# A fused linear-attention and GEGLU block on one core: the first forms of the down projection loaded ahead of two blocks of Wd, the last group's sums in an order of their own, and closings spread with their stores a step later

## The chip, the cores and the metric

The kernel runs on 1 core of a Trainium2 chip. The metric is device time in microseconds (us) of one execution; the times below are the median of 3 runs and their range. The profile is one execution taken by the hardware profiler. Its engines are PE (TensorE matmul; PEld is its weight load), DVE (VectorE), ACT (ScalarE), POOL (GpSimd) and SP (SyncE, which here only issues DMAs).

## The reference

```python
def _A_ref(x, wqkv, wo):            # linear attention, 32 heads of 18
    q, k, v = split_heads(x @ wqkv)
    phi = lambda t: jnp.where(t > 0, t + 1, jnp.exp(t)) + 1e-6
    pq, pk = phi(q), phi(k)
    kv = jnp.einsum("bhsd,bhse->bhde", pk, v)
    z = jnp.einsum("bhsd->bhd", pk)
    num = jnp.einsum("bhqd,bhde->bhqe", pq, kv)
    den = jnp.einsum("bhqd,bhd->bhq", pq, z)[..., None] + 1e-6
    return merge_heads(num / den) @ wo

def _B_ref(x, w_gate, w_up, w_down):
    h = gelu(x @ w_gate) * (x @ w_up)
    return h @ w_down

xn = layernorm(x)                   # x: 2048 x 576, hidden width 4608
return x + _A_ref(xn, ...) * silu(_B_ref(xn, ...))
```

All operands are float32.

## The kernel before

Every float32 product is made of several matmuls on a rounded operand ("hi", written by ACT) and its remainder ("lo", written by DVE as source minus hi).

The program has four stages, one after the other: k and v, then q and the attention output (both up to about 303 us of the profiled execution), then the gate and up matrices, then the down projection. The change lies in the last step of the third stage and in the fourth.

**Gate and up.** A matrix is done in seven block products (`al`, `be`, `ga`, `de`, `al`, `ga`, `de`, line 738), each over two halves of the tokens. Two matrices of two steps each form a *macro group*; there are nine (`NM`), numbered `m` = 0 to 8. A macro group leaves 16 products `h`. They and the sums live in 17 buffers of 128x512, called spots: eight in four `spot_h` tiles, three in `spot_m`, six in `spot_g`. From the products 28 sums are formed on POOL, by the table `ADDS`: an entry `(v, a, b, sign, at)` makes value `v` from `a` and `b`, not before hook `at` of the group. `add_up` (line 827) writes over an operand that nobody needs any more, or takes the spot that came free first. The 26 values named in `FORM` are the *forms*, which are stored to memory (`hs_d`); for the last macro group these stores are issued by POOL itself, right behind the add (`put_out`, line 819), for the others by SP.

**Down projection.** It is done in 26 *passes* (`PROD`). Pass `p` multiplies one form of all nine macro groups (nine steps `kt`) with one combination of blocks of Wd and adds into four PSUM banks: 9 x 4 x 3 = 108 matmuls of 128x288 a pass. The nine steps are cut into five *units* `k` (two steps each, the last one step: macro group 8, which is stored last). Per unit and in this order, `down_all` (line 1135) writes the program: load a third of a Wd block (`load_reg`, passes in `LOADS`), form combinations of Wd blocks on DVE (`change`), split the next pass's weights into hi and lo (`make_words`: ACT, then DVE, tiles `w_head` and `w_end`), split the unit two ahead into hi and lo (`cut`: ACT, then DVE in place on `raw_a`, `raw_b`, `raw_h` or `raw_g`), the matmuls (`down_mm`), then the loads of the same unit for the next pass (`load_unit`, 256 KB each), and in unit 1 the reading of the last pass's banks (`read`). The eight Wd blocks are called by two digits (`"22"`, `"42"`, `"32"`, `"12"`, ...); in the trace a whole one is a `b<-in_wd_dram` load.

**Start of the down projection.** `down_first` (line 1120) lists, for the seven steps of the last up matrix, what is put behind each: four whole blocks of Wd, then the loads of the five units of pass 0, the weights of pass 0 and the first cuts.

**Closings.** Where an output block is complete (`ENDS`: passes 9, 13, 19, 21, 22 twice, 24, 25), `close` does a SiLU on ACT, a multiply and an add on DVE (tile `sx`) and a store to the output, for each of four 128-row parts. From unit 2 of the next pass on, up to three parts are closed a unit. (`run(list, n)` takes the first `n` entries off a list and calls them.)

**Order.** All instructions are kept in the order in which the program writes them on their engine. SP is one queue too: a load whose buffer, source or predecessor isn't ready holds all loads and stores behind it.

Of the kernel before, what the change touches and what calls it, by code (L numbers as in the profile page):

```python
# [49 lines left out]
NM = NG // 2  # L50
# [3 lines left out]
ADDS = (  # L54
# [7 lines left out]
)  # L62

FORM = (33, 18, 11, 19, 31, 27, 29, 15, 30, 25, 6, 43, 40, 42, 35, 17, 4, 26, 39, 24, 41, 22,
# [18 lines left out]
def block_kernel(ctx, tc, x, xe, wq_d, wkv_d, wo, wgu_d, wd_d, out):  # L83
# [12 lines left out]
    def big(i, shape, dt, name):  # L96
        return sb.tile(shape, dt, tag=f"b{i}", bufs=1, name=name)
# [15 lines left out]
    def act(*args, **kw):  # L113
        pin(nc.scalar.activation(*args, **kw))  # L114

    def vec(op, *args, **kw):
        pin(getattr(nc.vector, op)(*args, **kw))  # L117
# [7 lines left out]
    def dma(out, in_, eng=None):  # L125
        tc.keep_in_program_order((eng or nc.sync).dma_start(out=out, in_=in_))
# [277 lines left out]
    def run(todo, n=None):  # L404
        for _ in range(len(todo) if n is None else min(n, len(todo))):
            todo.pop(0)()
# [53 lines left out]
    at = {}  # L460
# [363 lines left out]
    def later(at, f):  # L824
        events.setdefault(at, []).append(f)

    def add_up(m, v, a, b, sign, at):
        into = next((x for x in (a, b) if left[m, x] == 1), None)
        va, vb = value(m, a), value(m, b)
        born(m, v, None if into is None else place_of[m, into])  # L830
        pool("tensor_add" if sign > 0 else "tensor_sub", value(m, v), va, vb)
        for x in (a, b):
            used(m, x, at + 0.5, keep=x == into)
        if v in FORM:
            put_later(m, v, at)
# [7 lines left out]
    def run_events(at):  # L843
        for f in events.pop(at, []):
            f()

    def open_macro(m):
        for v, a, b, sign, at in ADDS:
            at += HOOKS * m
            later(at, lambda a=(m, v, a, b, sign, at): add_up(*a))  # L850

# [50 lines left out]
    def load_reg(at, nm, third=None):  # L902
        if at not in reg:
            b = big(REG[at], [P, REG_W], F32, f"b_{at}")
            reg[at] = b[:, 0 : KT * HALF].rearrange("p (k d) -> p k d", k=KT)
        j, c = int(nm[0]) - 1, int(nm[1]) - 1
        par, f = divmod(KP[j], 2)
        src = wd_d[par::2, :, f, c * HALF : (c + 1) * HALF].rearrange("g p d -> p g d")
        k = slice(0, KT) if third is None else slice(3 * third, 3 * third + 3)
        dma(out=reg[at][:, k], in_=src[:, k])  # L910
# [6 lines left out]
    def raw_place(p, k):  # L917
        if p < 4:
            if k in (0, 1, 4):
                t = ring("a", lambda: big(15, [P, 5, TBN], F32R, "raw_a"))  # L920
            else:
                i = 10 if p == 0 else 6
                t = ring(("b", i), lambda: big(i, [P, 5, TBN], F32R, f"raw_b{i}"))
            return t[:, 4:5] if k == 4 else t[:, 2 * (k % 2) : 2 * (k % 2) + 2]
        if k == 4:
            return ring(("g", p % 2), lambda: gl_tile([P, 1, TBN], f"raw_g{p % 2}", F32R))
        return ring(("h", k), lambda: slot([P, 2, TBN], F32R, f"raw_h{k}"))

    def load_unit(p, k):
        if p >= NP:  # L930
            return
        raw_v[p, k] = v = raw_place(p, k)
        for i in range(*UNITS[k]):
            dma(out=v[:, i - UNITS[k][0]].bitcast(F32), in_=hs_d[i][:, PROD[p][0]])
# [4 lines left out]
    def hi_place(p, k):  # L939
        if k == 4 and p > 2:  # L940
            return ring(("hg", p % 2), lambda: gl_tile([P, 1, TBN], f"hi_g{p % 2}", F32R))
        i = 2 if k == 4 else (4 * p + k) % 3
        if i == 2 and k < 4:
            return beside()[:, 0 : 2 * TBN].rearrange("p (k t) -> p k t", k=2)
        t = ring("hi", lambda: big(0, [P, 5, TBN], F32R, "hi"))
        return t[:, 4:5] if k == 4 else t[:, 2 * i : 2 * i + 2]

    def cut(u):
        p, k = divmod(u, NU)
        if p >= NP:  # L950
            return
        hi, lo = hi_place(p, k), raw_v[p, k]
        hi_v[p, k] = hi
        src = lo.bitcast(F32)
        act(hi, src, AF.Copy)
        vec("tensor_sub", lo, src, hi.bitcast(F32))
# [3 lines left out]
    def word_tiles(p):  # L960
# [34 lines left out]
    }  # L995

    LOADS = {
# [3 lines left out]
    }  # L1001
# [1 line left out]
    def change(p, c):  # L1003
        for nm, a, op, b in CHANGES.get(p, ()):
            r = [reg[x][:, HALVES[c]] for x in (nm, a, b)]
            vec("tensor_add" if op == "+" else "tensor_sub", *r)
# [34 lines left out]
    def acc_of(o):  # L1041
        i, j = ACCS[o]
        if i not in acc_t:
            acc_t[i] = big(i, [P, 2, TT, HALF], F32, f"acc_{i}")
        return acc_t[i][:, j]
# [21 lines left out]
    def places(o):  # L1067
        i, c = divmod(o, 2)
        tb = TP[i]
        cols = slice(c * HALF, (c + 1) * HALF)  # L1070
        rows = lambda j: slice(tb * TBN + j * P, tb * TBN + (j + 1) * P)
        return tb, cols, rows

    def load_sx(o):
# [7 lines left out]
        else:  # L1082
            sxs[o] = [tmp([P, 2, HALF], f"sx_{o}_{j}") for j in range(TT)]
            for j, t in enumerate(sxs[o]):
                dma(out=t[:, 0], in_=s_d[tb][:, j, cols])
                dma(out=t[:, 1], in_=x[rows(j), cols])

    def close(o, j):
        _, cols, rows = places(o)
        y, t = acc_of(o)[:, j], sxs[o][j]  # L1090
        act(y, y, AF.Silu, scale=float(SIGN[o]))
        vec("tensor_mul", t[:, 0], y, t[:, 0])
        vec("tensor_add", t[:, 0], t[:, 0], t[:, 1])
        dma(out=out[rows(j), cols], in_=t[:, 0])

    def close_last(o, j, p, parts):

# [22 lines left out]
    def down_first():  # L1120

        return [
            [lambda: load_reg("22", "22")],
            [lambda: load_reg("42", "42")],
            [lambda: load_reg("32", "32"), lambda: load_reg("12", "12")],
            [lambda: load_unit(0, 0), lambda: load_unit(0, 1), lambda: make_words(0, 0)],
            [
                lambda: load_unit(0, 2), lambda: load_unit(0, 3), lambda: load_unit(0, 4),
                lambda: make_words(0, 1), lambda: cut(0),
            ],  # L1130
            [lambda: cut(1)],
            [],
        ]

    def down_all():
        late = []
        last = NP - 1
        for u in range(NP * NU):
            p, k = divmod(u, NU)
            n = KT * p + 2 * k  # L1140
            for at in sorted(events):
                if at <= H_END + n // 2:
                    run_events(at)
            if p in LOADS and k < 3:
                load_reg(*LOADS[p], k)
            if k == 0:
                for o, e in ENDS.items():
                    if e == p:
                        load_sx(o)
            if k < 2:  # L1150
                change(p + 1, k)
            elif k < 4:
                make_words(p + 1, k - 2)
            cut(u + 2)
            if p == last and k == 2:
                break
            for kt in range(*UNITS[k]):
                down_mm(p, kt, range(TT))
            load_unit(p + 1, k)
            if k == 1 and p:  # L1160
                read(p - 1)
                late += [
                    lambda o=o, j=j: close(o, j) for o, e in ENDS.items() if e == p - 1
                    for j in range(TT)
                ]
            elif k > 1:
                run(late, 3)
        run(late)
        o = next(o for o, e in ENDS.items() if e == last)
        for j in range(TT):  # L1170
            for kt in range(UNITS[2][0], KT):
                down_mm(last, kt, (j,))
            late += close_last(o, j, last, 2 if j == TT - 1 else 1)
            run(late, len(late) - 1)
        run(late)
# [97 lines left out]
    for n in range(3, 2 * TT):  # L1273
# [3 lines left out]
        if n >= TT:  # L1277
            j, c = divmod(n - TT, 2)
# [165 lines left out]
```

## Time and profile before

| | us |
|---|---|
| median of 3 runs | 1499.71 |
| range of the runs | 1496.04 to 1501.43 |
| the profiled execution | 1498.64 |
| its span | 1496.7 |
| PE busy (share of the span) | 1473.3 (98%) |
| DVE busy | 1145.1 (77%) |
| POOL busy | 600.7 (40%) |
| ACT busy | 560.8 (37%) |

A timeline row has the start in us, the duration in us, engine, line, operation, output and inputs, shape and count, and in brackets how long the engine sat idle before it and what ended that. A row of windows has a stretch, its length, the busy time of engines with their instruction counts, the granted PE clock as a share of full speed, the mean busy share of the DMA engines and GB/s.

### The profile page before, as it was taken

What the parts mean: (1) busy time and instruction counts of PE and PEld (TensorE: products, weight loads), DVE (VectorE), ACT (ScalarE), POOL (GpSimd) and SP (SyncE); (2) the same over time, 40 slices, a digit from 0 to 9 for tenths busy, and PEclk for the clock granted to TensorE, in tenths of its full rate; (3) what the DMA queues carried; (4) which work ended last, traced back from release to release, by engine and by line L of the source; (5) the groups of instructions that cost most, each with busy time, mean ns of one, the idle gap of its engine ahead of it and who ended that gap; (6) DMA issues with size and microseconds to landing.
All of it is one profiled execution on the core that took longest, in us unless ns stands there. A gap on an engine that the chain in (4) does not pass through costs nothing.

```text
span 1496.7 us, 21860 instructions
## 1 busy us (share of the span) xinstructions
PE 1473.3 (98%) x8128; PEld 1310.3 (88%) x8128; DVE 1145.1 (77%) x1574; ACT 560.8 (37%) x923; POOL 600.7 (40%) x528
## 2 busy tenths in 40 slices
PE   8999999999999999999999999999999999999997
PEld 7989988988888888888888888888878999999997
DVE  7567466546778788777878878777876978989887
ACT  5434335433223222223233232332234556545553
POOL 4342241125655757655675755667636000000000
PEclk9999999999999999999999999999999999999999
DMA  4425004452242423333152243314297888767875
GB/s 169 181 109 207 6 2 158 150 199 85 92 134 81 145 85 117 123 113 134 50 176 91 92 148 106 119 72 166 81 313 251 279 254 262 240 181 233 291 266 204
DMA packets 115100, 230.62 MB, mean 154 GB/s; under 512 B 10850, under 2 KB 42850, under 8 KB 112946
## 3 DMA queue, kind: packets, MB, share of 16 engines
q1 hardware_dynamic: 112338, 217.17, 42.8%
q0 software_dynamic: 2656, 12.06, 2.1%
q8 instruction: 64, 1.05, 0.3%
q14 instruction: 42, 0.34, 0.1%
HBM read 146.57 MB, written 82.58 MB: 153 GB/s over the span
## 4 chain that ended last, share of the span: by engine, by line
PE 92%; DVE 3%; DMA 2%; POOL 1%; issue 1%; ACT 1%; SPq 0%; DVEq 0%; ACTq 0%; POOLq 0%
PE bd L120 22%; PE ga L738 14%; PE de L738 14%; PE al L738 14%; PE kv L120 8%; PE be L738 7%; PE q L120 4%; PE s L120 4%; DMA raw_a<-hs 1%; PE kv_a L120 1%; PE xt L197 1%; PE d L120 1%; DVE sx L117 1%; DMA hs<-spot_g 0%; DVE acc L117 0%
## 5 line engine op out<-in xcount | busy, mean ns | idle before, releaser
L123 POOL TENSOR_TENSOR sm<-raw 128x384 f32<-128x384 f32 x72 | 76.1, 1057 | 153.5 <-DMA raw<-in_wgu_dram 137.5
L120 PE MATMUL kv<-wkv,xo_B 128*128 128x384 f32 x672 | 126.3, 343 | 1.8 <-POOL wkv L123 0.9
L120 PE MATMUL bd<-w_head,hi 128*128 128x288 f32 x516 | 120.3, 299 | 3.3 <-ACT hi L114 3.3
L117 DVE TENSOR_TENSOR wa<-sm,wa 128x768 fp32r<-128x768 f32 x72 | 93.0, 1292 | 36.1 <-ACT wa L114 35.2
L120 PEld LDWEIGHTS kv<-wkv,xo_B 128*128 128x128 f32 x672 | 117.5, 190 | 3.5 <-POOL wkv L123 1.6
L117 DVE TENSOR_TENSOR wb<-raw,wb 128x256 fp32r<-128x256 f32 (+1 forms) x108 | 106.1, 982 | 7.3 <-ACT wb L114 5.8
L117 DVE TENSOR_TENSOR wa<-raw,wa 128x256 fp32r<-128x256 f32 x72 | 65.0, 903 | 50.7 <-ACT wa L114 47.5
L114 ACT ACTIVATE hi<-raw_h 128x1024 fp32r<-128x1024 f32 x59 | 62.5, 1060 | 97.5 <-PE bd L120 65.5
L120 PEld LDWEIGHTS bd<-w_head,hi 128*128 128x128 f32 x516 | 88.7, 192 | 4.0 <-ACT hi L114 4.0
L120 PE MATMUL bd<-w_end,hi 128*128 128x288 f32 x448 | 89.9, 294 | 0.0
L117 DVE TENSOR_TENSOR raw_h<-raw_h,hi 128x1024 fp32r<-128x1024 f32 x59 | 71.7, 1221 | 22.9 <-ACT hi L114 22.8
L114 ACT ACTIVATE spot_h<-spot_h 128x512 f32<-128x512 f32 x49 | 30.8, 633 | 151.6 <-DVE spot_h L117 151.6
L120 PE MATMUL bd<-w_end,raw_h 128*128 128x288 f32 x264 | 77.9, 295 | 0.0
L114 ACT ACTIVATE u<-al 128x512 f32<-128x512 f32 x72 | 41.0, 592 | 90.1 <-PE al L738 77.6
L114 ACT ACTIVATE wa<-sm 128x1152 fp32r<-128x1152 f32 x36 | 41.8, 1161 | 83.5 <-PE de L738 81.3
L120 PEld LDWEIGHTS bd<-w_end,hi 128*128 128x128 f32 x448 | 71.8, 188 | 0.0
L120 PE MATMUL bd<-beside,raw_h 128*128 128x288 f32 x240 | 70.9, 295 | 0.1
L123 POOL TENSOR_TENSOR spot_h<-spot_h,spot_h 128x512 f32<-128x512 f32 x46 | 63.9, 1395 | 2.9 <-DVE spot_h L117 2.4
L120 PE MATMUL q<-xo_B,wq 128*128 128x512 f32 x240 | 64.1, 395 | 0.0
L738 PE MATMUL ga<-xo_B,wb 128*128 128x512 f32 x252 | 63.2, 390 | 0.5 <-DVE u L117 0.5
L738 PE MATMUL al<-xo_B,wa 128*128 128x512 f32 x252 | 63.0, 389 | 0.0
L738 PE MATMUL ga<-xr_B,wb 128*128 128x512 f32 x252 | 63.0, 389 | 0.0
(247 smaller groups left out, 4097.3 us busy)
## 6 DMA issues: line engine op xcount, KB each, us to landing
raw_h<-hs SPq DMA_DIRECT2D x176, 256.0 KB
raw<-in_wgu_dram SPq DMA_DIRECT2D x36, 768.0 KB
hs<-spot_h SPq DMA_DIRECT2D x90, 256.0 KB
hs<-spot_g SPq DMA_DIRECT2D x80, 256.0 KB
b<-in_wd_dram SPq DMA_DIRECT2D x39, 432.0 KB
hs<-spot_m SPq DMA_DIRECT2D x38, 256.0 KB
raw_g<-hs SPq DMA_DIRECT2D x22, 256.0 KB
b<-in_wd_dram SPq DMA_DIRECT2D x4, 1296.0 KB
```

Source lines behind the costliest of these rows:

```text
L114: pin(nc.scalar.activation(*args, **kw))
L117: pin(getattr(nc.vector, op)(*args, **kw))
L120: pin(nc.tensor.matmul(*args, **kw))
L123: pin(getattr(nc.gpsimd, op)(*args, **kw))
L197: pin(nc.tensor.transpose(xts[n][j][:, k, :], xs[:, j, k * P : (k + 1) * P], ident))
L738: nc.tensor.matmul(o, w[0:rows, wi, :], xop[0:rows, xi, :], start=(start and n == 0), stop=(n == len(PASSES) - 1), skip_group_check=True,)
```

## The change

It has three parts.

1. Two of the four whole Wd blocks leave the head of the SP queue. Block `"32"` (one load) now comes behind the nine loads of pass 0; block `"12"` comes as three thirds in the first three units of pass 1.
2. The last macro group takes its sums from `ADDS_LAST`: the first 14 entries as before, the other 14 in another order and with other hooks.
3. At most two parts are closed a unit, from unit 2 on and also in unit 0 of the following pass; the store of a closed part is put on a list and issued at the end of the next unit, behind that unit's loads.

```diff
+ADDS_LAST = ADDS[:14] + (
+    (28, 14, 22, 1, 27), (25, 11, 20, 1, 29), (35, 7, 25, -1, 29), (21, 14, 15, 1, 30),
...
+)
...
     def open_macro(m):
-        for v, a, b, sign, at in ADDS:
+        for v, a, b, sign, at in ADDS_LAST if m == NM - 1 else ADDS:
...
     LOADS = {
-        2: ("31", "31"), 3: ("41", "41"), 4: ("11", "11"), 5: ("21", "21"),
+        1: ("12", "12"), 2: ("31", "31"), 3: ("41", "41"), 4: ("11", "11"), 5: ("21", "21"),
...
+    stores = []
+
     def close(o, j):
...
-        dma(out=out[rows(j), cols], in_=t[:, 0])
+        stores.append(lambda: dma(out=out[rows(j), cols], in_=t[:, 0]))
...
             [lambda: load_reg("22", "22")],
             [lambda: load_reg("42", "42")],
-            [lambda: load_reg("32", "32"), lambda: load_reg("12", "12")],
+            [],
...
-            [lambda: cut(1)],
+            [lambda: load_reg("32", "32"), lambda: cut(1)],
...
             load_unit(p + 1, k)
+            run(stores)
             if k == 1 and p:
                 read(p - 1)
...
-            elif k > 1:
-                run(late, 3)
+            else:
+                run(late, 2)
         run(late)
+        run(stores)
```

PE executes the same instructions in the same order as before. On SP, at the end of the gate and up stage, the queue before, from the first Wd block to the last load of pass 0 (`hs_79` to `hs_87` are the stored forms of macro groups 0 to 8):

```order
L126 DMA b_8700<-in_wd_dram 128x9x288
L126 DMA b_8720<-in_wd_dram 128x9x288
L126 DMA b_8742<-in_wd_dram 128x9x288
L126 DMA b_8744<-in_wd_dram 128x9x288
L126 DMA raw_a<-hs_79 128x512
L126 DMA raw_a<-hs_80 128x512
L126 DMA raw_a<-hs_81 128x512
L126 DMA raw_a<-hs_82 128x512
L126 DMA raw_b_8792<-hs_83 128x512
```

and of the change:

```order
L134 DMA b_8700<-in_wd_dram 128x9x288
L134 DMA b_8720<-in_wd_dram 128x9x288
L134 DMA raw_a<-hs_79 128x512
L134 DMA raw_a<-hs_80 128x512
L134 DMA raw_a<-hs_81 128x512
L134 DMA raw_a<-hs_82 128x512
L134 DMA raw_b_8788<-hs_83 128x512
L134 DMA raw_b_8788<-hs_84 128x512
L134 DMA raw_b_8788<-hs_85 128x512
L134 DMA raw_b_8788<-hs_86 128x512
L134 DMA raw_a<-hs_87 128x512
L134 DMA b_8820<-in_wd_dram 128x9x288
```

Two whole blocks went from ahead of the first unit to behind the last; one of them (`b_8820`) is seen here, the other follows in thirds.

On POOL, in the last macro group, the sums 23, 40, 25 and 35 with their stores, before (35 is the form that the last unit of pass 2 loads):

```order
L123 TENSOR_TENSOR spot_g_3001<-spot_g_3001,spot_g_2996 128x512
L126 DMA hs_87<-spot_g_3001 128x512
L123 TENSOR_TENSOR spot_g_3001<-spot_m,spot_g_3001 128x512
L126 DMA hs_87<-spot_g_3001 128x512
L123 TENSOR_TENSOR spot_h_2992<-spot_h_2992,spot_g_2999 128x512
L126 DMA hs_87<-spot_h_2992 128x512
L123 TENSOR_TENSOR spot_m<-spot_m,spot_h_2992 128x512
L126 DMA hs_87<-spot_m 128x512
```

and of the change the sums 27, 28 (not stored), 25 and 35:

```order
L131 TENSOR_TENSOR spot_h_2993<-spot_m,spot_h_2993 128x512
L134 DMA hs_87<-spot_h_2993 128x512
L131 TENSOR_TENSOR spot_h_2994<-spot_g_2996,spot_h_2994 128x512
L131 TENSOR_TENSOR spot_g_2997<-spot_h_2992,spot_g_2999 128x512
L134 DMA hs_87<-spot_g_2997 128x512
L131 TENSOR_TENSOR spot_g_2997<-spot_m,spot_g_2997 128x512
L134 DMA hs_87<-spot_g_2997 128x512
```

The store of 35 stood seventh among the stores behind that of 27 and now stands second; 35 is now written into the spot from which 25 has just been stored.

On DVE, in pass 14, around the cut of the first unit of pass 15 (`raw_h` with `hi`), before:

```order
L117 TENSOR_TENSOR sx_1_10746<-sx_1_10746 128x288
L117 TENSOR_TENSOR sx_2_10747<-acc_9218,sx_2_10747 128x288
L117 TENSOR_TENSOR sx_2_10747<-sx_2_10747 128x288
L117 TENSOR_SCALAR w_end_8771<-b_8744,w_end_8771 128x1152
L117 TENSOR_TENSOR raw_h_9328<-raw_h_9328,hi 128x1024
L117 TENSOR_TENSOR sx_3_10748<-acc_9218,sx_3_10748 128x288
```

and of the change:

```order
L125 TENSOR_TENSOR sx_1_10748<-sx_1_10748 128x288
L125 TENSOR_SCALAR w_end_8767<-b_8997,w_end_8767 128x1152
L125 TENSOR_TENSOR raw_h_9330<-raw_h_9330,hi 128x1024
L125 TENSOR_TENSOR sx_2_10749<-acc_9220,sx_2_10749 128x288
L125 TENSOR_TENSOR sx_2_10749<-sx_2_10749 128x288
L125 TENSOR_TENSOR sx_3_10750<-acc_9220,sx_3_10750 128x288
```

The third part's multiply and add went from ahead of that cut to behind it.

3 rows, old and new, of the table ADDS_LAST are left out of this document.

## The prediction, made before the changed kernel was run

> **What bounds the kernel now.** I read the waits of TensorE first, from the last up matrix to the end.
>
> ```profile
> span 1496.7 us, 21860 instructions
> PE bd L120 <- ACT hi L114: 3.3, 2, 2.0
> PE bd L120 <- DVE raw_h L117: 3.3, 3, 2.0
> PE bd L120 <- DVE raw_a L117: 2.4, 4, 0.7
> PE bd L120 <- DVE raw_b L117: 1.0, 1, 1.0
> ```
>
> TensorE is the bound: in the last 404 us it waits only 10.0 us. Nothing ahead of that stretch is edited, so the change can win back these 10.0 us and what hangs on them. The timeline of TensorE says where they lie:
>
> ```profile
> 1101.83 1.75 PE L738 MATMUL de<-xr_T,wb 128*128 128x512 f32 x7
> 1104.93 0.53 PE L120 MATMUL bd<-w_head,hi 128*128 128x288 f32 x2 [1.35 <-ACT hi L114]
> 1106.19 0.40 PE L120 MATMUL bd<-w_head,raw_a 128*128 128x288 f32 x1 [0.73 <-DVE raw_a L117]
> 1109.98 0.40 PE L120 MATMUL bd<-w_head,raw_a 128*128 128x288 f32 x1 [0.34 <-DVE raw_a L117]
> 1114.40 0.40 PE L120 MATMUL bd<-w_head,raw_b 128*128 128x288 f32 x1 [0.97 <-DVE raw_b L117]
> 1150.24 0.40 PE L120 MATMUL bd<-w_end,raw_a 128*128 128x288 f32 x1 [0.59 <-DVE raw_a L117]
> 1153.82 0.85 PE L120 MATMUL bd<-w_head,hi 128*128 128x288 f32 x2 [1.99 <-ACT hi L114]
> 1155.37 0.61 PE L120 MATMUL bd<-w_head,raw_a 128*128 128x288 f32 x1 [0.71 <-DVE raw_a L117]
> 1330.33 0.40 PE L120 MATMUL bd<-w_head,raw_h 128*128 128x288 f32 x1 [0.97 <-DVE raw_h L117]
> 1461.34 0.40 PE L120 MATMUL bd<-w_head,raw_h 128*128 128x288 f32 x1 [2.05 <-DVE raw_h L117]
> 1465.06 0.40 PE L120 MATMUL bd<-w_head,raw_h 128*128 128x288 f32 x1 [0.27 <-DVE raw_h L117]
> ```
>
> There are three places. At the start of the down projection, right behind the last up matrix (which ends at 1103.58), 1.35 + 0.73 + 0.34 + 0.97 = 3.39 us. At the end of pass 2 and start of pass 3, 0.59 + 1.99 + 0.71 = 3.29 us. At passes 15 and 24, 0.97 and 2.05 + 0.27 us. The second place costs more than its waits, as the windows of TensorE show:
>
> ```profile
> 1145.00:1150.00 5.00, 4.65 (x35) 1.00 0.72 238
> 1150.00:1155.00 5.00, 2.44 (x12) 0.82 1.01 359
> 1155.00:1160.00 5.00, 4.63 (x19) 0.50 1.05 405
> 1340.00:1450.00 110.00, 110.00 (x833) 1.00 0.83 268
> ```
>
> Undisturbed, a matmul takes 110/833 = 0.132 us, a pass of 108 of them 14.26 us. In the 15 us from 1145 on, 66 were done, worth 8.7 us; 6.3 us were lost, of which 3.3 us were waits. The other 3.0 us are the clock, which was granted at 0.50 behind the wait.
>
> **Part 1, two blocks of Wd leave the head of the queue.** These rows show why the first unit is late:
>
> ```profile
> b<-in_wd_dram SPq DMA_DIRECT2D x4, 1296.0 KB
> 1084.57 6.75 SPq L126 DMA_DIRECT2D b<-in_wd_dram  x4
> 1084.50:1094.00 9.50, 1.00 0.92 311
> 1094.14 2.09 SPq L126 DMA_DIRECT2D raw_a<-hs  x4
> 1104.00:1106.00 2.00, 1.00 1.05 404
> 1103.82 1.06 ACT L114 ACTIVATE hi<-raw_a 128x1024 fp32r<-128x1024 f32 x1 [10.89 <-DMA raw_a<-hs]
> 1098.20 1.35 DVE L117 TENSOR_TENSOR w_end<-b,w_end 128x1152 fp32r<-128x1152 f32 x1
> ```
>
> Four blocks of 1.33 MB are 5.31 MB; by 1094.0 9.5 us x 311 GB/s = 2.95 MB had moved. So when `raw_a` is issued at 1094.14, 2.36 MB still lie ahead of it, at 404 GB/s 5.8 us; by whole blocks, 2.65 MB are taken away, 6.6 us. The unit landed at 1103.8 and will land at 1097.2 to 1098.0. VectorE is at `w_end` until 1099.55 anyhow and then cuts the unit (the first cut ran from 1104.91, so 1.2 us): ready at 1100.8, 2.8 us ahead of TensorE. The next deadline is the third unit, 4 x 12 matmuls = 6.3 us behind the start: 1109.9. VectorE's order up to it stands in these two rows:
>
> ```profile
> 1108.71 1.22 DVE L117 TENSOR_TENSOR raw_a<-raw_a,hi 128x1024 fp32r<-128x1024 f32 x1
> 1112.50 1.85 DVE L117 TENSOR_TENSOR raw_b<-raw_b,beside 128x1024 fp32r<-128x1024 f32 x1
> ```
>
> Behind the first cut (end 1106.1 before) the second cut began 2.6 us later, and from there to the end of the third cut took 5.6 us. From 1100.8 that makes 1109.0: 0.9 us to spare. So all 3.39 us go; the bounds are 2.5 (this margin is missed by as much) and 3.39. The moved loads cost TensorE nothing: block 32 lies in front of the first unit of pass 1, whose matmuls begin at 1103.58 + 14.26 = 1117.8. All that is queued by then (what is left of the nine loads of pass 0, 2.36 MB in all, and 1.33 MB) takes 3.69/0.404 = 9.1 us from 1094.2, to 1103.4. Block 12 is first needed in pass 3. Uncovered, a block would cost its 3.3 us.
>
> **Part 2, the order of the last sums.** These rows carry the second stall:
>
> ```profile
> SPq L126 <- DMA hs<-spot_m: 9.7, 1, 9.7
> 1145.23 0.32 SPq L126 DMA_DIRECT2D raw_a<-hs  x1
> 1119.19 0.56 POOL L126 DMA_DIRECT2D hs<-spot_h  x1 [0.30 <-POOL spot_h L123]
> 1131.85 0.56 POOL L126 DMA_DIRECT2D hs<-spot_g  x1 [0.57 <-POOL spot_g L123]
> 1136.04 2.06 POOL L123 TENSOR_TENSOR spot_g<-spot_m,spot_g 128x512 f32<-128x512 f32 x1 [3.64 <-DMA hs<-spot_g]
> 1142.83 0.56 POOL L126 DMA_DIRECT2D hs<-spot_m  x1 [0.30 <-POOL spot_m L123]
> 1109.09 0.54 POOL L126 DMA_DIRECT2D hs<-spot_g  x1 [12.92 <-DVE spot_g L117]
> ```
>
> SP reached the last load of pass 2 at 1145.23 - 9.7 = 1135.5 and stood until the store of sum 35, issued at 1142.83, had landed 2.4 us later. Every load of pass 3 was queued behind it. In the new order, behind the store of 27 (1119.19 to 1119.75) come 28 and 25 at 1.4 us, 0.3 us and the store of 25 at 1122.8. Sum 35 is written over 25's spot, so it waits for that store to land: a wait that is new. Row 1136.04 is of this kind, 4.2 us behind its store's issue at 1131.85. So 35 starts at 1127.0, takes 2.1 + 0.3, is issued at 1129.4 and has landed by 1131.8. SP asks for it 3.4 us earlier than before, at 1132.1. Moreover, POOL's first store (1109.09) waited 12.9 us for VectorE, which was held by the first cut; that cut is over some 5.3 us sooner, so 35 lands nearer to 1126.5. The stall of 3.29 us goes, and with it the 3.0 us of low clock. Bounds: the waits 2.7 to 3.29, the clock 0 to 3.0.
>
> By the Trainium skill, page "TensorE: Matmul & The Clock Gate", Part 1, the clock halves after about one idle window of 3.4 us. No single wait here is longer than 1.99 us, so by that rule these waits wouldn't have halved it, and the low stretch could stay; the row has the half clock right behind them, and I go by the row.
>
> What POOL does last moves too, 42 and 29 behind 26 and 30; its wait of 3.64 us on a store (row 1136.04) has a like one at 35, so its end is sooner by the 5.3 us alone. Pass 4's weights and fourth unit wait for the last two stores (a rival below).
>
> **Part 3, the closings.** VectorE is the releaser at passes 15 and 24:
>
> ```profile
> 1325.20 0.45 DVE L117 TENSOR_TENSOR sx<-acc,sx 128x288 f32<-128x288 f32 x1
> 1325.68 0.46 DVE L117 TENSOR_TENSOR sx<-sx 128x288 f32<-128x288 f32 x1
> 1442.87 1.23 DVE L117 TENSOR_TENSOR raw_h<-raw_h,beside 128x1024 fp32r<-128x1024 f32 x1 [2.40 <-ACT beside L114]
> 1460.06 1.22 DVE L117 TENSOR_TENSOR raw_h<-raw_h,hi 128x1024 fp32r<-128x1024 f32 x1
> ```
>
> One closing occupies VectorE 0.86 us (1325.20 to 1326.06). Before pass 15 one less lies ahead of the cut: 0.97 becomes 0.11. Before pass 24 VectorE works without a gap from 1442.87, when it had waited for a load, to the cut at 1460.06. Between them lay 1 + 3 closings, and now 2 + 2: the one saved below is handed in above, and the 2.05 us stay. The cut behind it has two closings ahead instead of three, and the 0.27 us go. Gain 0.86 + 0.27 = 1.1 us, bounds 0 (the closings of unit 0 get in the way of pass 24's later cuts) and 3.3. The stores cost SP the same issues, now behind loads that need not wait for VectorE; the output isn't read again.
>
> **Sum.** 3.39 + 3.29 + 3.0 + 1.1 = 10.8 us. Against the profiled execution, 1498.64, that gives 1487.8. The median shown, 1499.71, is 1.1 us above it, so I forecast 1488.9.
>
> **Rivals.**
> 1. *The clock dip stays or comes elsewhere.* For it: no dip follows the 3.39 us at 1104, so a wait alone doesn't decide it. Against: it begins at the longest wait. The 3.0 us are lost: 1491.9.
> 2. *VectorE becomes the bound in pass 0.* Its margin at the third unit is 0.9 us, and POOL now works in the same microseconds; the same cut took 1.22 and 1.85 us above. If the early start is used up in later waits, 3.39 us are lost, 1492.3.
> 3. *The change doesn't do what it says at sum 35:* SP still stands because of its own new wait, or another late store. Then only 3.39 + 1.1 us come: 1495.2.
> 4. *Slower: pass 4's weights on VectorE.* They are written over the spot of 42, whose store is now the last but one. Even with POOL no earlier than before (its last stores ran to 1155), it is issued by 1153 and lands at 1157; then VectorE needs 1.6 + 0.7 + 1.35 + 1.2 = 4.9 us to the first cut of pass 4, due at 1103.6 + 4 x 14.26 = 1160.6. That is a stall of 1.3 us; POOL 5.3 us earlier, none. It decides only when the store lands over 8 us later still, at 1165: a stall of 9.3 and a low clock of 3.0 exceed the gain. At 1168, 12.3 + 3.0 - 10.8 = 4.5 us slower, 1504.2.
>
> **How the numbers follow.** The forecast 0.60, rival 1 0.15, rival 2 0.13, rival 3 0.07, rival 4 0.05. A measurement of this kernel can tell about 0.3%, 4.5 us, from no change. The forecast and the first two rivals are faster by more; rival 3 lies on the border and is halved: faster 0.91, and with some doubt in my rows 0.89; same 0.06; slower 0.05. The forecast's own range is 1486 to 1491. For 8 in 10, it goes up to 1495.0, which takes in the first two rivals; down to 1485.0, with the 2.05 us gone too and 1.5 us for the spread of the runs shown.
>
> **What would show it.** The first `bd` matmul follows the last `de` without a wait; `hi` of the first unit starts near 1098. The last load of pass 2 isn't held by a store, TensorE has no wait at pass 3, and no window between 1145 and 1165 has a clock of 0.50. The wait at pass 24 is still some 2 us, that of pass 15 about 0.1. Wrong it is if waits of TensorE between 1104 and 1165 still sum to over 2 us, or if the clock falls anywhere else in the down projection.

## The result and the profile after

The changed kernel took 1488.87 us, the median of six runs (1486.08 to 1494.1), against 1500.44 us for the kernel before, six runs beside it (1496.04 to 1501.94): ratio 0.9928, 95% interval 0.9904 to 0.9952. The forecast was 1488.9, the range 1485.0 to 1495.0. The six runs stand in two groups and one outlier: 1486.08, 1486.27, 1486.83; 1490.91, 1491.02; 1494.1. The profiled execution is the one of 1491.02 us, so it shows the changed kernel on one of its worse runs. This is its summary of TensorE's waits in the same stretch as before (us in total, times, longest), and then its timeline:

```profile
span 1489.3 us, 21859 instructions
PE bd L128 <- DVE raw_a L125: 3.3, 2, 2.6
PE bd L128 <- DVE raw_h L125: 2.1, 1, 2.1
```

```profile
1101.87 1.75 PE L746 MATMUL de<-xr_T,wb 128*128 128x512 f32 x7
1103.46 0.42 PE L128 MATMUL bd<-w_head,hi 128*128 128x288 f32 x2
...
1135.09 0.40 PE L128 MATMUL bd<-beside,raw_a 128*128 128x288 f32 x1 [2.61 <-DVE raw_a L125]
1151.90 0.40 PE L128 MATMUL bd<-w_head,raw_a 128*128 128x288 f32 x1 [0.71 <-DVE raw_a L125]
1454.92 0.40 PE L128 MATMUL bd<-w_head,raw_h 128*128 128x288 f32 x1 [2.09 <-DVE raw_h L125]
```

The waits fell from 10.0 us to 5.4. The first one after the last `de` is gone, and so are 0.97 at pass 15 and 0.27 in pass 24. But two stand where the forecast has none: 2.61 us inside pass 2 (which runs from about 1132 to 1151) and 0.71 at the start of pass 3, 3.32 us in all, as much as the 3.29 us that were to vanish there. Behind the first of them the clock falls. These windows show all five engines, in the order PE, PEld, DVE, ACT, POOL, and then the clock, the DMA share and GB/s:

```profile
1130.00:1135.00 5.00, 2.48 (x19) 2.24 (x17) 5.00 (x3) 1.06 (x1) 4.06 (x6) 1.00 0.88 291
1135.00:1140.00 5.00, 4.91 (x25) 4.91 (x26) 4.48 (x3) 0.29 (x1) 4.36 (x5) 0.66 0.80 288
```

A mean of 0.66 over 5 us, between 1.00 and 0.50, is 0.34/0.5 x 5 = 3.4 us at half clock. Before, it was 0.18/0.5 x 5 = 1.8 us in one window and all 5 us of the next, 6.8 us at the second stall. VectorE, the third of these columns, works without a pause from 1130 to 1135 while TensorE stands: the new wait is VectorE's.

**The head of the queue.** SP now issues two blocks of Wd instead of four ahead of the first unit, as the timeline shows:

```profile
1084.61 3.55 SPq L134 DMA_DIRECT2D b<-in_wd_dram  x2
1094.18 2.28 SPq L134 DMA_DIRECT2D raw_a<-hs  x4
1099.15 1.06 ACT L122 ACTIVATE hi<-raw_a 128x1024 fp32r<-128x1024 f32 x1 [5.94 <-DMA raw_a<-hs]
1100.24 1.22 DVE L125 TENSOR_TENSOR raw_a<-raw_a,hi 128x1024 fp32r<-128x1024 f32 x1 [0.65 <-ACT hi L122]
1107.83 1.84 DVE L125 TENSOR_TENSOR raw_b<-raw_b,beside 128x1024 fp32r<-128x1024 f32 x1
```

`hi` of the first unit starts at 1099.15 (1103.82 before; forecast 1098), and its cut ends at 1101.46, 2.0 us ahead of TensorE. The cut of the third unit ends at 1109.67, where 1109.0 was forecast and 1109.9 was the limit; TensorE does not wait there.

**The sums.** On POOL and SP:

```profile
1104.42 0.54 POOL L134 DMA_DIRECT2D hs<-spot_g  x1 [8.21 <-DVE spot_g L125]
1122.13 2.34 POOL L131 TENSOR_TENSOR spot_g<-spot_m,spot_g 128x512 f32<-128x512 f32 x1 [3.57 <-DMA hs<-spot_g]
1124.77 0.56 POOL L134 DMA_DIRECT2D hs<-spot_g  x1 [0.30 <-POOL spot_g L131]
1132.25 0.32 SPq L134 DMA_DIRECT2D raw_a<-hs  x1
```

The second row is sum 35 in 25's old spot, behind the landing of 25's store, the third its store: it went out at 1124.77 where 1142.83 was before. SP issues the last load of pass 2 at 1132.25, in its turn (1145.23 before, held 9.7 us). So the held queue is gone, as forecast.

**Where the new wait is from.** The three instructions of VectorE that lead up to the wait at 1135.09, with POOL's adds of the same microseconds; first the kernel before, then the change, then a second execution of the same changed kernel (the run after_third below):

```profile
1132.73 0.68 DVE L117 TENSOR_TENSOR raw_a<-raw_a,hi 128x512 fp32r<-128x512 f32 x1
1133.33 1.35 DVE L117 SCALAR_TENSOR_TENSOR w_end<-b,w_end 128x1152 fp32r<-128x1152 f32 x1
1134.60 1.21 DVE L117 TENSOR_TENSOR raw_a<-raw_a,beside 128x1024 fp32r<-128x1024 f32 x1
```

```profile
1125.36 3.99 POOL L131 TENSOR_TENSOR spot_g<-spot_g,spot_g 128x512 f32<-128x512 f32 x2
1128.11 1.78 DVE L125 TENSOR_TENSOR raw_a<-raw_a,hi 128x512 fp32r<-128x512 f32 x1
1129.82 2.93 DVE L125 SCALAR_TENSOR_TENSOR w_end<-b,w_end 128x1152 fp32r<-128x1152 f32 x1
1130.22 1.30 POOL L131 TENSOR_TENSOR spot_g<-spot_g,spot_h 128x512 f32<-128x512 f32 x1
1132.67 2.36 DVE L125 TENSOR_TENSOR raw_a<-raw_a,beside 128x1024 fp32r<-128x1024 f32 x1
```

```profile
1121.04 1.28 POOL L131 TENSOR_TENSOR spot_g<-spot_m,spot_g 128x512 f32<-128x512 f32 x1 [2.71 <-DMA hs<-spot_g]
1127.37 1.77 DVE L125 TENSOR_TENSOR raw_a<-raw_a,hi 128x512 fp32r<-128x512 f32 x1
1129.07 1.34 DVE L125 SCALAR_TENSOR_TENSOR w_end<-b,w_end 128x1152 fp32r<-128x1152 f32 x1
1129.74 1.82 POOL L131 TENSOR_TENSOR spot_h<-spot_h,spot_h 128x512 f32<-128x512 f32 x1
1130.34 2.30 DVE L125 TENSOR_TENSOR raw_a<-raw_a,beside 128x1024 fp32r<-128x1024 f32 x1
1132.69 0.40 PE L128 MATMUL bd<-beside,raw_a 128*128 128x288 f32 x1 [0.73 <-DVE raw_a L125]
```

Before, these three took 0.68, 1.35 and 1.21 us, because POOL stood still from 1132.4 to 1136.0 (the 3.64 us in the row at 1136.04 of the prediction). The new order moved POOL's pause to 1118.6 to 1122.1, ahead of VectorE's work, and the same three took 1.78, 2.93 and 2.36: 3.8 us more, each longer by about an add of POOL's. In the third fence it is the add that waits, 1.82 instead of 1.30, `w_end` takes 1.34, and TensorE waits 0.73 instead of 2.61. The Trainium skill, page "SBUF — State Buffer", section "Who interferes with whom", says that a VectorE instruction with two SBUF inputs contends with a GpSimd instruction that reads SBUF, that the ports they share are an exclusive lock, and that the issue order decides who waits. The rows agree with the lock: 1.35 against 2.93 on one side, 1.30 against 1.82 on the other. The order can't always be read from where a row starts: in the change the row of `w_end` starts at 1129.82, ahead of that of the add at 1130.22, and `w_end` is the one stretched.

**What it costs in one view.** Windows of the whole disputed stretch, 1104 to 1165, of the kernel before, of the change, and of after_third:

```profile
1104.00:1165.00 61.00, 54.75 (x383) 53.23 (x384) 46.66 (x33) 29.19 (x41) 36.47 (x37) 0.94 0.78 265
```

```profile
1104.00:1165.00 61.00, 57.68 (x423) 57.21 (x422) 51.08 (x35) 30.00 (x42) 37.72 (x37) 0.97 0.94 321
```

```profile
1104.00:1165.00 61.00, 60.27 (x454) 59.80 (x453) 54.24 (x36) 31.02 (x43) 36.86 (x36) 1.00 0.95 325
```

At 0.1325 us a matmul, 61 us hold 460. Before, 77 are missing, 10.2 us; in the profiled run of the change 37, 4.9 us; in after_third 6, 0.8 us. Between the last two lie 4.1 us. The two groups of the six runs lie 4.5 us apart, but that this is the same difference isn't shown: after_third as a whole took 1489.22 us, between the groups, since it lost time again in pass 24 (below), and no profiled execution is of the lower group.

### The profile page after: what moved, and what is told of

Same layout as the page of the kernel before. It is cut to its first block, busy times and chain, and to the rows that moved or that the text cites. A ratio compares the mean times of both kernels' runs of the same rounds, so it can differ in the third digit from the quotient of the medians.

```text
span 1489.3 us, 21859 instructions
## 1 busy us (share of the span) xinstructions
PE 1470.5 (99%) x8128; PEld 1309.2 (88%) x8128; DVE 1146.2 (77%) x1574; ACT 560.4 (38%) x923; POOL 602.3 (40%) x528
## 4 chain that ended last, share of the span: by engine, by line
PE 93%; DVE 4%; DMA 1%; issue 1%; ACT 0%; POOL 0%; SPq 0%; DVEq 0%; ACTq 0%; POOLq 0%
PE bd L128 22%; PE ga L746 15%; PE de L746 15%; PE al L746 15%; PE kv L128 8%; PE be L746 7%; PE q L128 4%; PE s L128 4%; PE kv_a L128 1%; PE xt L205 1%; PE d L128 1%; DMA raw_h<-hs 0%; DVE w_end L125 0%; DVE raw_h L125 0%; DVE acc L125 0%
```

## The experiments

Each run was timed beside the kernel before on the same chip. Medians, ratios with their 95% interval, and from each profiled execution the matmuls done from 1104 to 1165 and from 1445 to 1465, with the granted clock there (20 us hold 151 matmuls). The down projection starts 1.5 us later in the profile of sums_only than before, 0.9 in closings_only and 0.6 in no_adds, so their counts from 1104 on are a few too low:

| run | median us (range, runs) | ratio | 1104:1165 | 1445:1465 |
|---|---|---|---|---|
| before (beside the next four) | 1499.14 (28 runs) | | 383, 0.94 | 132, 1.00 |
| after_again | 1487.25 (1485.82 to 1491.98, 6) | 0.993 [0.9914, 0.9945] | 438, 1.00 | 122, 0.91 |
| loads_only | 1495.48 (1492.58 to 1498.41, 11) | 0.9978 [0.9968, 0.9987] | 422, 0.97 | 139, 1.00 |
| sums_only | 1498.97 (1495.7 to 1501.06, 12) | 0.9998 [0.9989, 1.0007] | 385, 0.97 | 132, 1.00 |
| closings_only | 1497.56 (1496.23 to 1499.88, 12) | 0.9992 [0.9984, 1.0001] | 382, 0.97 | 135, 1.00 |
| no_adds | 1487.04 (1486.22 to 1487.65, 4) | 0.9921 [0.9907, 0.9934] | 452, 1.00 | 137, 1.00 |
| cut_first | 1485.54 (1485.16 to 1488.39, 5) | 0.9916 [0.9903, 0.993] | 455, 1.00 | 140, 1.00 |
| pause_later | 1487.09 (1486.29 to 1489.74, 5) | 0.9924 [0.9912, 0.9937] | 454, 1.00 | 126, 0.91 |
| best | 1483.98 (1483.49 to 1484.24, 4) | 0.990 [0.9887, 0.9914] | 460, 1.00 | 147, 1.00 |
| loads_sums | 1490.03 (1489.0 to 1493.16, 5) | 0.994 [0.9927, 0.9954] | 450, 1.00 | 124, 0.91 |
| after_third | one run, 1489.22 | | 454, 1.00 | 122, 0.91 |
| after_fourth | one run, 1488.89 | | 438, 1.00 | 137, 1.00 |
| before_again | one run, 1499.43 | | 388, 0.94 | 121, 0.93 |

The kernel before took 1499.57 us (9 runs) beside no_adds, cut_first, pause_later and best, and 1499.13 (9 runs) beside loads_sums and the last three.

### The whole change again, and each part alone

after_again is the changed kernel as it is.

> The changed kernel once more, for a second profile and five more times. Theory A (VectorE is stretched by GpSimd's last adds): its first cut of pass 2 is again 2 to 3 us late in the profile (TensorE waits 2.6 us at about 1135 us) in every run, and the times lie near 1489, with 2 to 5 us of spread from how long the clock stays low behind that wait. Rival B (the wait at 1135 us was a chance of that one execution): this profile has no wait of TensorE between 1104 and 1165 us, and the time is near 1486.

Its median is 11.9 us below the kernel before, and its profiled run (1490.49 us) has the wait in pass 2 once more, 2.75 us, with `w_end` at 2.92 us, as theory A has it. The median, 1487.25, lies between the times of the two theories. There is no low clock behind it, but one of 3.4 us in pass 24 (20 us at 0.91).

loads_only is the kernel before with part 1:

```diff
-        2: ("31", "31"), 3: ("41", "41"), ...
+        1: ("12", "12"), 2: ("31", "31"), 3: ("41", "41"), ...
-            [lambda: load_reg("32", "32"), lambda: load_reg("12", "12")],
+            [],
-            [lambda: cut(1)],
+            [lambda: load_reg("32", "32"), lambda: cut(1)],
```

> Only part 1 of the change, the two Wd blocks moved. The first 3.4 us of waits go. Theory A: GpSimd's last sums come 5 us sooner, so the store of sum 35 lands at about 1140 us, in time or nearly; GpSimd's pause of 3.6 us falls at 1127 to 1131 us instead of 1132 to 1136, and part of VectorE's words for pass 2 run beside adds: TensorE waits 0 to 2.5 us at pass 2 or 3. Gain 5 to 9 us. Rival (part 2 is what removes the stall at pass 3, as I forecast): that stall stays whole, 6.3 us with the clock, and the gain is 3.4 us.

It gains 3.7 us, as the rival had it, not theory A. Its profile is of its fastest execution (1492.58 us). There the first waits are gone, and the late store of 35 still holds SP (timeline of loads_only):

```profile
1128.18 1.34 DVE L117 SCALAR_TENSOR_TENSOR w_end<-b,w_end 128x1152 fp32r<-128x1152 f32 x1
1132.02 1.28 POOL L123 TENSOR_TENSOR spot_g<-spot_m,spot_g 128x512 f32<-128x512 f32 x1 [4.76 <-DMA hs<-spot_g]
1140.45 0.32 SPq L126 DMA_DIRECT2D raw_a<-hs  x1
1145.45 0.40 PE L120 MATMUL bd<-w_end,raw_a 128*128 128x288 f32 x1 [0.19 <-DVE raw_a L117]
1148.71 0.53 PE L120 MATMUL bd<-w_head,hi 128*128 128x288 f32 x2 [1.66 <-ACT hi L114]
1150.59 0.61 PE L120 MATMUL bd<-w_head,raw_a 128*128 128x288 f32 x1 [1.36 <-DVE raw_a L117]
```

POOL pauses until 1132.0, `w_end` takes 1.34 in the pause, and pass 2 has no wait: the stall stays at pass 3, 0.19 + 1.66 + 1.36 = 3.2 us, where the kernel before has it.

sums_only is the kernel before with the table `ADDS_LAST` and its use in `open_macro` alone.

> Only part 2, the order of the last sums. The first 3.4 us of waits stay. As forecast: the stall at pass 3 with its low clock goes, 6.3 us faster. Theory A: the hold of the load queue goes, but GpSimd now adds without a pause at 1127 to 1137 us, where VectorE makes the words and first cuts of pass 2, and these take twice as long; TensorE waits 2 to 4 us there, so the gain is only 0 to 4 us.

Nothing is gained: 1498.97, within the 0 to 4 us of theory A. This is the run that shows the exchange most clearly (timeline of sums_only, of its slowest execution, 1501.06 us; its line numbers are one lower than the change's):

```profile
1135.69 2.94 DVE L124 SCALAR_TENSOR_TENSOR w_end<-b,w_end 128x1152 fp32r<-128x1152 f32 x1
1136.09 1.31 POOL L130 TENSOR_TENSOR spot_g<-spot_g,spot_h 128x512 f32<-128x512 f32 x1
1138.55 2.36 DVE L124 TENSOR_TENSOR raw_a<-raw_a,beside 128x1024 fp32r<-128x1024 f32 x1
1140.96 0.40 PE L127 MATMUL bd<-beside,raw_a 128*128 128x288 f32 x1 [2.66 <-DVE raw_a L124]
```

The stall at pass 3 shrinks to 0.70 us, since SP isn't held, and 2.66 us stand in pass 2, where the adds run beside VectorE: 3.36 us instead of 3.29. The low clock behind the wait is 3.4 us instead of 6.8; counted over 61 us from the end of the last up matrix (1105.12 here, 1103.58 before), TensorE did 389 matmuls instead of 381, 1.1 us more. The medians differ by 0.2 us.

closings_only is the kernel before with part 3:

```diff
+    stores = []
...
-        dma(out=out[rows(j), cols], in_=t[:, 0])
+        stores.append(lambda: dma(out=out[rows(j), cols], in_=t[:, 0]))
...
+            run(stores)
...
-            elif k > 1:
-                run(late, 3)
+            else:
+                run(late, 2)
...
+        run(stores)
```

> Only part 3, the closings. Nothing changes before pass 10. As forecast: the waits at pass 15 (0.97 us) and the second at pass 24 (0.27 us) go, the 2.05 us stay, 1.1 us faster; from the profile after the change, where the last pass too came 0.7 us sooner, up to 1.9 us. Rival: the stores behind the loads cost as much as the closings save, no difference.

It measured 1.6 us less, with an interval that reaches to no change; the forecast was 1.1. The wait at pass 15 is gone and that of pass 24 is 2.11.

### Parts 1 and 2 together

loads_sums is the change with the closings as they were (`dma` at once, `elif k > 1: run(late, 3)`).

> Parts 1 and 2 without the closings. Alone they gave 3.7 and 0.2 us. If parts simply add, 1495.3. As forecast for the two together (3.39 for the first wait, 6.3 for the stall at pass 3): 1489.6. Theory A by the profiles of the changed kernel (2.6 to 3.3 us of waits come back at pass 2): 1490 to 1493.

1490.03: 9.1 us below its kernel before (1499.13). So the sums, worth 0.2 us alone, are worth 9.1 - 3.7 = 5.4 us on top of part 1, by a difference of medians whose intervals leave some 2.5 us either way. In its profile, pass 2 has one wait of 1.23 us, `w_end` takes 1.35 us, nothing stands at pass 3, and the clock is 1.00 throughout 1104 to 1165. From 1104 to 1165 it did 28 matmuls more than the profiled loads_only, 3.7 us; where the rest of the 5.4 lies the profiles don't show. With the 1.6 us of part 3 alone that makes 10.7; the whole measured 11.6 and 11.9.

### Is it the adds?

no_adds is the change without POOL's last 16 sums: the condition on the hook takes out the 14 that have an order of their own, and 31 and 27 ahead of them. Their spots are stored as they lie:

```diff
-        pool("tensor_add" if sign > 0 else "tensor_sub", value(m, v), va, vb)
+        if m < NM - 1 or at < HOOKS * m + 27:
+            pool("tensor_add" if sign > 0 else "tensor_sub", value(m, v), va, vb)
```

> The changed kernel without GpSimd's last 14 additions; the values that they would make are stored as they lie there, so all stores stay and the output is not the reference's. Theory A (an addition on GpSimd stops VectorE for about its own 1.3 us): VectorE's words and first cuts of pass 2 take 1.2 to 1.8 us each instead of 2.3 to 2.9, TensorE has no wait between 1104 and 1165 us, and the clock is not lowered there; 2 to 5 us faster than the changed kernel, about 1484.5. Rival (GpSimd's issue of stores, or the loads of the moved Wd blocks, slow VectorE or delay the first unit of pass 2): the operations stay long and TensorE waits 2 us or more at pass 2.

```profile
1130.09 0.68 DVE L125 TENSOR_TENSOR raw_a<-raw_a,hi 128x512 fp32r<-128x512 f32 x1
1130.69 1.35 DVE L125 SCALAR_TENSOR_TENSOR w_end<-b,w_end 128x1152 fp32r<-128x1152 f32 x1
1132.79 1.22 DVE L125 TENSOR_TENSOR raw_a<-raw_a,beside 128x1024 fp32r<-128x1024 f32 x1 [0.75 <-ACT beside L122]
1134.07 0.40 PE L128 MATMUL bd<-beside,raw_a 128*128 128x288 f32 x1 [0.73 <-DVE raw_a L125]
```

In this timeline of no_adds the durations are back at 0.68, 1.35 and 1.22, with all stores still there: the adds stretched them. The time is 1487.04, not the 1484.5 expected, and no gain over after_again (1487.25). VectorE starts the series 2.7 us later than in after_third, and the 0.73 us that TensorE waits are now a load's: ACT stood 1.65 us for `raw_a` ahead of the cut. SP waits 1.0 us for one of POOL's stores, which go out in a burst here; that the stores make the loads late is not shown. All four runs are below 1488; four are too few to say that the group near 1491 is gone.

pause_later keeps all adds and puts POOL's pause back where VectorE needs it, with sums 25 and 35 behind 36, 43, 21 and 23:

```diff
-    (28, 14, 22, 1, 27), (25, 11, 20, 1, 29), (35, 7, 25, -1, 29), (21, 14, 15, 1, 30),
-    (23, 6, 21, 1, 30), (43, 6, 28, 1, 31), (36, 11, 32, -1, 31), (33, 21, 27, 1, 33),
+    (28, 14, 22, 1, 27), (36, 11, 32, -1, 29), (43, 6, 28, 1, 29), (21, 14, 15, 1, 30),
+    (23, 6, 21, 1, 30), (25, 11, 20, 1, 31), (35, 7, 25, -1, 31), (33, 21, 27, 1, 33),
```

> The changed kernel with sums 36, 43, 21 and 23 ahead of 25 and 35, so that GpSimd's pause (35 waits for the store of 25) falls at about 1126 to 1130 us, where VectorE makes the words and the first cut of pass 2, and the store of 35 lands at about 1135 us. Theory A: the wait of 2.7 us at pass 2 goes, none comes at pass 3 (SP is held 3 us by the store, but the loads behind it wait for TensorE anyhow); 2.5 to 4.5 us faster than the changed kernel, 1484 to 1486. Rival (it is the number of additions, not where the pause lies): no difference, 1487 to 1489.

```profile
1128.88 1.34 DVE L125 SCALAR_TENSOR_TENSOR w_end<-b,w_end 128x1152 fp32r<-128x1152 f32 x1
1130.14 1.21 DVE L125 TENSOR_TENSOR raw_a<-raw_a,beside 128x1024 fp32r<-128x1024 f32 x1
1132.43 1.29 POOL L131 TENSOR_TENSOR spot_h<-spot_m,spot_h 128x512 f32<-128x512 f32 x1 [4.48 <-DMA hs<-spot_h]
```

With the pause from 1127.95 to 1132.43 both run undisturbed, pass 2 has no wait, and 0.88 us remain at pass 3. So the waits are as theory A has them: the adds are all there, and where the pause lies decides. The time is the rival's: the median, 1487.09, is that of after_again within its spread. The profiled run lost time again in pass 24, with a wait of 1.87 us and 3.4 us of low clock behind it.

### The other order on VectorE, and the best version

In cut_first, `down_all` writes the cut of the unit two ahead in front of the split of the next weights, in units 2 and 3:

```diff
-            elif k < 4:
+            cut(u + 2)
+            if 1 < k < 4:
                 make_words(p + 1, k - 2)
-            cut(u + 2)
```

> The changed kernel with the cut of the unit two ahead written before the weights of the next pass, in units 2 and 3. Theory A: VectorE makes the first unit of pass 2 before w_end, 2.9 us sooner, so the wait of 2.7 us there falls to under 0.5; at pass 24 the cut comes 1.3 us sooner and 2.1 to 2.3 us become 0.8 to 1.0. 3 to 6 us faster than the changed kernel, 1483 to 1485. Rival: the weights become late in their turn (kt 5 of the next pass), the waits move there, no gain.

1485.54. The waits are 0.81 in pass 2 and 0.55 + 0.68 in pass 24 (2.09 in the change): the cut no longer stands behind `w_end`. The gain over after_again, 1.7 us, is smaller than the 3 to 6 us expected, and the two intervals overlap.

best joins cut_first and pause_later, and closes four parts a unit in pass 22:

```diff
-                run(late, 2)
+                run(late, 4 if p == 22 else 2)
```

> pause_later and cut_first together, and the four closings of the block that ends in pass 21 all done in unit 2 of pass 22, where VectorE stands for a load. No wait at pass 2; at pass 24 the cut comes 1.3 + 1.7 us sooner, so its wait of 2.1 us goes as well. 1481 to 1484, the fastest of all; if the closings of pass 22 don't go into the idle time, 0.8 us stay at pass 24.

1483.98, as expected, 15.6 us below its kernel before (1499.57); each of its four runs is below every run of the change. What its third edit, the closings in pass 22, gives was not run alone. Its timeline has one wait from 1104 on, and its chain of waits runs through TensorE alone, 2580 matmuls in 341.93 us, 0.1325 each:

```profile
1450.90 0.40 PE L128 MATMUL bd<-w_head,raw_h 128*128 128x288 f32 x1 [0.46 <-DVE raw_h L125]
```

```profile
1103.47 341.93 PE bd L128 x2580
```

### The change in two more executions, and the kernel before in one

after_third and after_fourth are the changed kernel once more, for their profiles, and before_again is the kernel before.

> The changed kernel a third time, for its profile: its times fall in two groups, about 1486.5 and 1491, and both profiles so far are of the slower. If this one is of the faster group, it should show what is missing there: theory A says a wait at pass 2 below 1 us or no low clock behind the waits, or both; rival: the same waits, and the difference lies before 1103 us.

> As the run before: a profile of the changed kernel, of either group.

> The kernel before a second time, for its profile: the waits at 1104 (3.4 us) and at pass 3 (3.3 us) are there again; the low clock behind the second may be one window of 3.4 us, two, or none, depending on the execution.

after_third was shown above: 0.73 us in pass 2, then 2.26 us and 3.4 us of low clock in pass 24. after_fourth has 1.12 us in pass 2 with `w_end` at 1.35, 1.70 at pass 3 and 1.87 in pass 24, and no low clock there. before_again repeats the waits of the kernel before, 1.30 + 0.73 at the start, 0.62 + 1.70 + 1.30 at pass 3, 0.96 and 2.61 behind, but not where the clock fell: a stretch of 3.4 us from 1107 on, behind the first two waits (1.00 there before), one of 3.4 us at pass 3, where it was 6.8, and one in pass 24.

So one program has two courses through pass 2. The fork is visible at sum 35, which starts when the store of 25 has landed, at nearly the same time as VectorE's cut of `raw_b`. That cut in the change and in after_third:

```profile
1122.09 1.23 DVE L125 TENSOR_TENSOR raw_b<-raw_b,hi 128x1024 fp32r<-128x1024 f32 x1 [2.15 <-ACT hi L122]
1121.57 1.83 DVE L125 TENSOR_TENSOR raw_b<-raw_b,hi 128x1024 fp32r<-128x1024 f32 x1 [3.02 <-ACT hi L122]
```

In the change the cut began at 1122.09 and POOL's sum at 1122.13; the sum waited (2.34 us instead of 1.28), and all that followed on POOL lay 1 us later, on top of VectorE's series. In after_third the sum began first, at 1121.04, and came through in 1.28, and the cut was the one stretched. So it is in the other three: in after_again the cut led by 0.03 us and the sum took 2.35, in after_fourth and loads_sums the sum led by 0.17 and 0.06 us and took 1.29 and 1.28. after_again shows the first course, after_fourth, loads_sums and after_third the second. Two profiles of the change on each side do not give the odds.

## Why the prediction was right, and where its steps were not

**Part 1: right, in mechanism and size.** 3.39 us were forecast; the four first waits are gone in every profile that has it, and alone it measured 3.7 us. Its weakest term, the 0.9 us of margin at the third unit, shrank to 0.2 us but held.

**Part 2: the step "The stall of 3.29 us goes, and with it the 3.0 us of low clock" was not what happened.** Its first half held: 35 is stored 18 us earlier, behind a wait of 3.57 us like the row it was taken from, and SP isn't held. What failed is the sentence behind it, that POOL's wait of 3.64 us "has a like one at 35, so its end is sooner by the 5.3 us alone": the pause was taken as a delay of POOL and its move costed at nothing. It was also the one gap in which VectorE worked undisturbed. In sums_only the 3.29 us came back as 3.36; in the profiled run of the change as 3.32, with 3.4 us at half clock instead of the 6.8 before. By the prediction's own test (waits of more than 2 us between 1104 and 1165) the step fell in three of the four profiled executions of the change: 3.32, 2.75 and 2.82 us. In the other, after_third, the waits are 0.73 us, but its second sign of being wrong is there, a clock that falls elsewhere, in pass 24. So by the signs that it named itself the account was wrong in each of the four. The 3.0 us of clock, moreover, were read from one execution: before_again lost half as much at the same place (3.4 us at half clock, 1.7 us).

**Why the number came out all the same.** The sum held 6.3 us for this part. Measured on top of part 1 it is 5.4; alone it is 0.2. In part this is the other course, where only 0.7 to 1.2 us stand in pass 2 (with 1.70 at pass 3 in one of the three profiles) and the clock did not fall in the stretch. The parts do not add: 3.7 + 0.2 + 1.6 = 5.5 against 11.6 to 11.9. The profiled run, 1491.02, lies 2.1 us above the forecast, the lower three of the six some 2.5 below. That the median agrees with 1488.9 to 0.03 us is luck: VectorE's loss, which was put at nothing, cost 2.61 and 2.75 us of waits in pass 2 in two profiled executions of the change and 0.73 and 1.12 in the other two, and the six runs lie on both sides of the forecast.

**Part 3: its waits went as forecast, its time is not clear of noise.** 0.97 at pass 15 and 0.27 in pass 24 are gone, and 2.09 stays. (The 0.27 can't be put down to the closings for certain: before_again and loads_sums, both without them, don't have it either.) VectorE's rows at pass 15:

```profile
1322.59 1.22 DVE L125 TENSOR_TENSOR raw_h<-raw_h,hi 128x1024 fp32r<-128x1024 f32 x1
1323.73 0.45 DVE L125 TENSOR_TENSOR sx<-acc,sx 128x288 f32<-128x288 f32 x1
```

The closing that lay ahead of the cut of pass 15 now follows it. 1.1 us was the term, 1.6 the measurement alone, with an interval that reaches to no change.

**The rivals.** Rival 1 (the dip comes elsewhere) was half true: a stretch of 3.4 us of low clock came in pass 2 in one profile of the change and in pass 24 in two, none in after_fourth. Its argument that no dip follows the waits at 1104 held for the one execution it was read from, not for before_again. Rival 2 named the right two engines, "POOL now works in the same microseconds", and the wrong pass and cause: in pass 0 VectorE had its margin, and it was part 2, not the early start, that set the adds against it. Rivals 3 and 4 did not occur: SP was on time at 1132.25, and in the profiled run TensorE never waits between 1152 and 1452 (in after_third once, 0.45 us at 1262).

**Open.** What lets the store of 25 land up to a microsecond sooner in one execution than in the next wasn't tried, nor what decides whether the clock falls behind a given wait. The profiled no_adds is 3.7 us above the profiled best: its waits, 0.73, 0.17 and 1.78 us against 0.46, account for 2.2 of it, and its last up matrix ends 0.75 us later (1104.22 against 1103.47), ahead of all that was changed; 0.7 stay open.

## What to carry to other kernels

A pause on one engine can be another engine's only undisturbed time: before moving it, list which instructions of the other engine ran inside it and what they take outside it. A rearrangement that hits its target can still leave the sum of the waits as it was, and a part that measures nothing alone can be worth its full price once another part has moved the engines against each other, so test parts in pairs too. When one program's runs stand in two groups, profile it several times before explaining any of them.

## What the runs showed of the hardware

VectorE and GpSimd hold each other up by about a whole instruction in these rows: `w_end` takes 1.35 us alone and 2.93 with an add, the cut of `raw_b` 1.23 or up to 2.32, sum 35 1.28 or 2.34. VectorE's operations of 0.69 us with an input in PSUM (`de`, `ga`) kept their 0.69 us, and POOL's issue of a store at 1104.42 left the cut beside it (from 1104.04) at 1.22.

The clock fell in stretches of 3.4 us, once of 6.8 (before), behind single waits of 1.99 us (before), 2.61 (the change) and 2.26 (after_third), and not behind 2.75 (after_again, pass 2). In before_again it fell behind 1.30 and 0.73 us (0.72 from 1105 to 1110); before, with 1.35 and 0.73 us at the same place, it did not (1.00). In pass 24 a wait of 1.87 us was followed by it in pause_later (20 us at 0.91), one of 1.87 in after_fourth was not (1.00). The Trainium skill, page "TensorE: Matmul & The Clock Gate", Part 1, gives a free-running window of 3413 ns; the length of these stretches, 3.4 us, agrees with that. Its advice in "Why this matters for your kernels", no gap over some 3 us, isn't enough here, where gaps of 2 us and less were followed by the half clock in some executions.
